# Delta rule and MoE in one kernel: three copies instead of four for a chunk's answers, halved last outputs, and a new order of issue

## The chip, the cores and the metric

The kernel runs on one core of a Trainium2 chip. The metric is the device time of one execution in microseconds (us); lower is better. Kernels are compared by medians over executions on the same chip. One execution was also recorded by the hardware profiler; it has a time of its own, and a span from its first to its last instruction.

## What is computed

The reference is a linear attention layer with the delta rule, followed by a two-layer MoE expert whose inputs are the attention's outputs:

```python
def _attn_ref(q, k, v, beta):                 # 4 batches, 8 heads, 768 tokens, 48 channels
    k_n = k / (np.linalg.norm(k, axis=-1, keepdims=True) + 1e-06)
    for t in range(S):
        y[:, :, t] = np.einsum('bhd,bhde->bhe', q[:, :, t], state)
        v_old = np.einsum('bhde,bhd->bhe', state, kt)
        state = state + bt[:, :, :, None] * np.einsum('bhd,bhe->bhde', kt, vt - v_old)
...
def _moe_ref(x, w_in, w_out):                 # 3072 tokens, 384 -> 2048 -> 384
    h = x @ w_in
    g = h - np.tanh(h)
    return (g @ w_out).astype(np.float32)
```

## The kernel before

**Tiling.** The 768 tokens of a sequence are cut into 24 chunks `s` of 32; the 4 batches lie in the four quadrants of 32 partitions. Four chunks make a group `g` for the triangular solve and also a window `w` of 512 tokens for the MoE, so there are six of each.

**The recurrent part.** For the first four chunks `head` (L469) forms products of keys on TensorE straight from an early load `kf`; for later chunks `score` (L500) forms them, with the queries' products beside them, from tiles `kc` or `kd`. `solve(g)` inverts the triangular system of a group on VectorE: a transpose (L538), a row of small operations, thirty pairs of multiply and add (L594, L596), a scaling (L599) and a transpose (L604) that gives `tt`. VectorE also scales the values of the first four chunks (`prep`, L621, `wv<-v`). `chain` then goes from chunk to chunk: keys against the state (L642), the solution applied (L663), its copy `u_sb` (L671), the state's update (L679, L706), the answers (L692). `output` brings a chunk's answers from two PSUM banks to `y_sb` in four copies of 32 partitions on ScalarE (L719), because the answer of quadrant `b` lies in quadrant `b^1` of bank `b%2`; TensorE transposes them (L729) into `psa`, and two reads of it (L733 on ScalarE, L735 on VectorE) leave the high and low parts in `xt`.

**The MoE.** A unit of `hidden` is nine matmuls (L838), one of `out_units` nine more (L888); between them `gate` runs two operations on ScalarE and two on VectorE. A unit covers 512 tokens, except that the first `F0` feature blocks of the first window are done in two halves of 256 tokens, so that they can begin when two chunks are there. The weights come as 16 pieces: loaded as `raw` and decoded by ScalarE and VectorE (L750, L773, L786, L789). For the first ten pieces TensorE forms the low part, in two halves per piece of a matmul on `c` (L795) and one on `w` (L796), which ScalarE copies out (L799).

**The order.** Python simulates the engines while it emits code. `Plan.run` picks the next operation by earliest start and due time, from tables of costs and the numbers at the file's end (`QUIRK`, `OPEN` and so on). Each engine then runs its instructions in the order they were emitted. Where the plan sees TensorE idle, `warm` emits a matmul on a tile of zeros (L356, `po<-wz`); it computes nothing. `burn` does the same at the very start with `BURN` small matmuls (L333). The plan also counts TensorE's instructions in blocks of 256 (`fetched`, `fetch`), starting from the number `taken`. Loads are issued by SyncE in the order of `FIRST`, the later weights by ScalarE's queue.

**The end.** `finish` copies the three banks of a window (ScalarE, VectorE, ScalarE; L907) into a tile `o` that has two buffers, and stores each with one DMA (L910).

Of the kernel before, what the change touches and what calls it, by code (L numbers as in the profile page):

```python
# [8 lines left out]
F32 = mybir.dt.float32  # L9
F32R = mybir.dt.float32r  # L10
# [20 lines left out]
KR = 112  # L31
SPLIT = ((0, 0), (0, 1), (1, 0))
HALF = (slice(0, 48), slice(64, 112))


class Null:
# [208 lines left out]


def act(n, psum=False):
    return (0.17 if psum else 0.19) + 0.82e-3 * n


# [9 lines left out]
def kernel(ctx: ExitStack, tc: tile.TileContext, kf, kq, vk, beta, w_in, w_out, const, out):  # L260
# [118 lines left out]
    def load_values(s):  # L379
        both = ld.tile([128, 2, H, D], F32, name="v", bufs=VS)  # L380
        nc.sync.dma_start(both, vk[s])
        v_of[s] = (both, transfer(plan.free["SP"], 384), rv.take())

    beta_of = {}
    rbt = Ring(2)
# [243 lines left out]
    def chain():  # L629
        for s in range(NS):  # L630
# [2 lines left out]
            g, r = divmod(s, 4)  # L633
            solution = lambda: made[s].t if s in made else None
            if s > 0:
                (_, t) = yield Op("PE", 0.68, (known(kd_of, s, 1), get(s, "v", 2), state[s - 1], rk), by - 8.0, "small", 128)
# [73 lines left out]
    def output(s, py, pyr, e):  # L710
# [2 lines left out]
        y_sb = at.tile([128, DM], F32, tag="uy", name="y_sb", bufs=UYS)  # L713
        yr = ruy.take()
        yv = y_sb.rearrange("p (h e) -> p h e", h=H)
        for b in range(4):
            if b:
                (_, t) = yield Op("ACT", act(DM, True), (e,), need(s) - 3.0)
            nc.scalar.copy(yv[quad[b]], py[quad[b ^ 1], b % 2])  # L719
# [8 lines left out]
        for ct in range(NC):  # L728
            nc.tensor.transpose(px[:, ct, :], y_sb[:, 128 * ct:128 * ct + 128], ident)  # L729
# [142 lines left out]
    def out_units(units):  # L872
        for w, f, part, z in units:
# [9 lines left out]
            count = NF + F0 if w == 0 else NF  # L883
            po = pos[w][0]
            gh, gr = gh_of.pop((w, f, z))
            for c in range(NC):
                for i, (a, b) in enumerate(SPLIT):
                    nc.tensor.matmul(po[c][:, part], wo[f][:, a, 128 * c:128 * c + 128], gh[:, b, :n],  # L888
                                     start=(f == 0 and i == 0 and z < 1), stop=(ended.get(w, 0) == count - 1 and i == 2),
                                     skip_group_check=True)  # L890
            gr.t = t
            ended[w] = ended.get(w, 0) + 1
            if ended[w] == count:
# [2 lines left out]
    ended = {}  # L896
    ros = Ring(2)

    def finish(w, e):
        po, por = pos[w]  # L900
        t = 0.0
        for c in range(NC):
            eng = ("ACT", "DVE", "ACT")[c]
            (_, t1) = yield Op(eng, act(T, True) if eng == "ACT" else dve(T), (e, ros, closed), start(w + 1) - 4.0)
            o = post[0].tile([128, T], F32, name="o", bufs=2)
            orr = ros.take()
            (nc.scalar.copy if eng == "ACT" else nc.vector.tensor_copy)(o, po[c])  # L907
            t = max(t, t1)
            (_, t2) = yield Op("SP", ISSUE, (Event(t1),), start(w + 1) - 4.0)
            nc.sync.dma_start(out[w, c], o)  # L910
            orr.t = transfer(t2, 256).t
        por.t = t
# [46 lines left out]
    return plan  # L959


QUIRK = {'piece13': 15, 'prep0': 3, 'output0': -1, 'out_units0.0.1': 73, 'decode9': -28, 'hidden0.-1.2': 35, 'vsub0': -27, 'piece15': 75, 'solve0': 8, 'solve1': 5, 'piece4': -8, 'score1': -14, 'hidden0.1.3': -45, 'gate0.1.3': 17, 'vsub1': 13, 'out_units0.-1.3': 40, 'piece6': -10, 'out_units0.-1.1': -5, 'score2': -8, 'mask2': 40, 'score4': -20, 'piece11': 32, 'hidden0.0.3': 17, 'piece9': -5, 'decode5': 62, 'gate0.1.0': -7, 'chain5': -24, 'vsub4': 5, 'out_units0.1.1': -13, 'piece14': 54, 'join5': 13, 'decode12': -37, 'hidden0.0.2': 12, 'mask4': -15, 'add3': -18, 'piece10': -5, 'join4': 35, 'prep2': -28, 'output1': -30, 'mask5': -28, 'score0': 7, 'gate0.-1.0': -35, 'piece5': -22, 'answer2': 4, 'decode3': -15, 'chain3': -25, 'output5': -8, 'decode14': -15, 'add6': -35, 'piece12': -38, 'piece8': -17, 'answer3': 68, 'score3': 0, 'chain6': -10, 'answer5': 45, 'join0': -5, 'mask1': 15, 'add5': 22, 'out_units0.0.0': -30, 'out_units0.1.3': 14, 'output6': 24, 'prep1': 8, 'add1': -28, 'gate0.1.1': -7, 'decode1': -20, 'decode10': 8, 'decode0': -5, 'answer1': -3, 'mask3': 0, 'piece7': -15, 'mask0': -5, 'add4': -15, 'answer0': 17, 'hidden0.-1.0': 0, 'answer7': 22, 'add2': 5, 'add0': -5, 'decode2': -10, 'output2': -10, 'decode11': -18, 'out_units0.1.2': 0, 'vsub7': -12, 'output3': -4, 'hidden0.0.0': -7, 'solve2': 2, 'hidden0.-1.1': 10, 'hidden0.1.2': 22, 'chain1': -27, 'join7': -2, 'prep5': -15, 'vsub2': -5, 'gate0.-1.2': 10, 'output4': 2, 'vsub3': -2, 'chain4': 20, 'decode15': -5, 'chain7': -5, 'decode4': -20, 'join3': 5, 'mask6': -8, 'out_units0.1.0': 20, 'hidden0.1.1': -5, 'score7': 7, 'gate0.0.0': -10, 'decode8': -2, 'triangle1': 20, 'join6': 10, 'hidden0.0.1': -10, 'score6': 2, 'output7': -2, 'vsub5': -18, 'prep4': 10, 'decode13': 20, 'gate0.0.1': -10, 'chain0': -5, 'join1': 20, 'gate0.0.2': -2}
# [3 lines left out]
OPEN, SECOND, EARLY, PITCH, SPREAD, URGENCY, FETCH, QUEUED, FILL, LEAD, STICK = 87.5, 184.8, 44.6, 80.0, 13.6, 0.012, 3.8, 3.0, 150.0, 18.4, 0.0  # L966
WARM, HOLD, GUARD, F0 = 90.0, 120.0, 0.28, 4
FIRST = ['f0', 'f1', 'f2', 'f3', 'b0', 'w0', 'w4', 'k2', 'k1', 'v2', 'k3', 'v3', 'k0', 'w3', 'b1', 'k4', 'k6', 'w1', 'w2', 'v0', 'k7', 'v1', 'k5']
WHIM, SEED = 0.0, 199030
FIRST_NEED, NEXT_NEED, EAGER, JOIN = 42.9, -27.4, -269.8, -52.4  # L970
LOW, SPARE, MARGIN = True, 10, 15.2
# [60 lines left out]
```

## Time and profile before

| what | value |
|---|---|
| median of 3 runs | 610.96 us (610.93 to 611.75) |
| the profiled execution's own time | 610.21 us |
| its span, first to last instruction | 608.5 us |
| TensorE matmul busy | 97% of the span |
| VectorE, ScalarE, GpSimd busy | 64%, 42%, 10% |
| granted TensorE clock, mean | 0.995 |

A row of the timeline has its start and duration in us, the engine and line, the operation, the tiles written and read, a count where instructions were merged, and in brackets the idle time before it with what ended it. TensorE's high busy share has two readings: some of it is the matmuls on zeros that the plan put where it expected to wait.

### The profile page before, as it was taken

To read this page: it belongs to the slowest core of one execution; us is meant where nothing else is said; L and a number is where in the kernel's file an instruction comes from. 1 tells how busy PE (TensorE), PEld (TensorE's weight loads), DVE (VectorE), ACT (ScalarE), POOL (GpSimd) and SP (SyncE) were. 2 spreads that over 40 slices of the span, in tenths; PEclk is the share of its full clock that TensorE was granted. 3 is DMA by queue.
4 is the path that set the end of the run, shared out by engine and by line. 5 is a ranking of instruction groups with operands and counts; after the bars stand their busy time and mean duration, and the time that the engine had idled before them with its cause. 6 is when DMAs were issued, how large, how long until landed. Compare 5 with 4: busy or idle time off the path is not lost.

```text
span 608.5 us, 21905 instructions
## 1 busy us (share of the span) xinstructions
PE 588.2 (97%) x9984; PEld 459.7 (76%) x9984; DVE 390.5 (64%) x826; ACT 257.9 (42%) x472; POOL 58.6 (10%) x60
## 2 busy tenths in 40 slices
PE   4799999999999999999999999999999999999996
PEld 3355677978788878778878778877788877788885
DVE  2988768898478986789334789732779733243323
ACT  2243877656354244353243433334444235432223
POOL 0111010001021031010011200000200000000000
PEclk9899999999999999999999999999999999999999
DMA  8842466533222133232032231021121000010001
GB/s 282 342 161 95 141 206 197 165 106 124 85 79 77 71 110 122 65 96 75 14 97 70 92 98 52 1 90 37 53 74 52 3 2 3 3 52 1 0 1 52
DMA packets 19436, 52.44 MB, mean 86 GB/s; under 512 B 2576, under 2 KB 2704, under 8 KB 19344
## 3 DMA queue, kind: packets, MB, share of 16 engines
q1 hardware_dynamic: 15840, 43.10, 20.9%
q10 hardware_dynamic: 3504, 7.95, 4.1%
q8 instruction: 78, 1.28, 0.8%
q14 instruction: 14, 0.11, 0.1%
HBM read 46.32 MB, written 4.72 MB: 84 GB/s over the span
## 4 chain that ended last, share of the span: by engine, by line
PE 89%; DVE 4%; ACT 3%; DMA 2%; issue 2%; ACTq 0%
PE ph L838 32%; PE po L888 31%; PE po L356 4%; PE psk L642 4%; PE psa L500 4%; PE psa L663 3%; PE psk L692 3%; PE psa L679 2%; PE ph L795 2%; PE psa L729 1%; DMA raw<-in_w_in 1%; ACT y_sb L719 1%; PE ph L679 1%; DMA kc<-in_kq 1%; DVE c L786 1%
## 5 line engine op out<-in xcount | busy, mean ns | idle before, releaser
L888 PE MATMUL po<-gh,w 128*128 128x512 f32 (+1 forms) x900 | 213.7, 387 | 0.3 <-DVE gh L865 0.3
L838 PE MATMUL ph<-xt,w 128*128 128x512 f32 (+1 forms) x900 | 213.2, 387 | 0.2 <-DVE tmp L594 0.2
L888 PEld LDWEIGHTS po<-gh,w 128*128 128x128 f32 x900 | 161.7, 188 | 34.3 <-DVE gh L865 0.6
L838 PEld LDWEIGHTS ph<-xt,w 128*128 128x128 f32 x900 | 161.4, 188 | 34.1 <-DVE tmp L594 0.7
L855 ACT ACTIVATE t<-ph 128x512 f32<-128x512 f32 (+1 forms) x100 | 58.1, 581 | 149.1 <-PE ph L838 138.3
L857 DVE TENSOR_TENSOR t<-ph,t 128x512 f32<-128x512 f32 (+1 forms) x100 | 66.8, 668 | 82.1 <-ACT t L855 81.8
L865 DVE TENSOR_TENSOR gh<-t,gh 128x512 fp32r<-128x512 f32 (+1 forms) x100 | 69.2, 692 | 42.4 <-ACT gh L863 41.2
L863 ACT CAST gh<-t 128x512 fp32r<-128x512 f32 (+1 forms) x100 | 60.4, 604 | 75.0 <-DVE t L857 37.0
L596 DVE TENSOR_TENSOR a<-a,tmp 128x30 f32<-128x30 f32 (+9 forms) x180 | 62.5, 347 | 5.1
L594 DVE TENSOR_TENSOR tmp<-a 128x30 f32<-128x30 f32 (+9 forms) x180 | 62.3, 346 | 4.7
L719 ACT COPY y_sb<-psk 32x384 f32<-32x384 f32 x96 | 45.2, 471 | 37.0 <-PE psk L692 36.0
L621 POOL TENSOR_TENSOR wv<-v,nt 128x768 f32<-128x768 f32 x20 | 30.8, 1543 | 213.7 <-PE psa L663 169.3
L356 PE MATMUL po<-wz 128*128 128x512 bf16 x148 | 38.0, 393 | 0.0
L517 POOL TENSOR_TENSOR pq<-pq,cs 128x256 f32<-128x256 f32 x24 | 19.3, 802 | 160.6 <-ACT pq L511 160.6
L735 DVE TENSOR_TENSOR xt<-psa,xt 128x384 fp32r<-128x384 f32 x24 | 13.3, 555 | 27.7 <-ACT xt L733 27.7
L642 PEld LDWEIGHTS psk<-st,kd 48*64 48x64 f32 x1472 | 23.6, 134 | 5.2 <-issue 4.2
L642 PE MATMUL psk<-st,kd 48*64 48x48 f32 x1472 | 26.4, 220 | 0.0
L356 PEld LDWEIGHTS <-wz 128*128 128x128 bf16 x148 | 13.3, 99 | 16.6 <-issue 3.7
L651 DVE TENSOR_TENSOR wv<-wv,psk 128x768 f32<-128x768 f32 x23 | 21.9, 951 | 5.2 <-PE psk L642 4.4
L663 PEld LDWEIGHTS psa<-wv,tt 32*32 32x32 f32 x1536 | 17.9, 105 | 8.6 <-issue 5.8
L679 PEld LDWEIGHTS psa<-u_sb,v 32*48 32x48 f32 x736 | 18.3, 119 | 7.9 <-issue 6.5
L500 PEld LDWEIGHTS psa<-kc 48*32 48x32 f32 x1344 | 19.4, 107 | 5.7 <-issue 3.9
(70 smaller groups left out, 454.6 us busy)
## 6 DMA issues: line engine op xcount, KB each, us to landing
kd<-in_kq SPq DMA_DIRECT2D x23, 512.0 KB, 3.5
kc<-in_kq SPq DMA_DIRECT2D x21, 512.0 KB, 4.0
v<-in_vk SPq DMA_DIRECT2D x24, 384.0 KB, 3.7
out<-o SPq DMA_DIRECT2D x18, 256.0 KB, 2.0
raw<-in_w_in ACTq DMA_DIRECT2D x5, 768.0 KB, 6.0
raw<-in_w_out ACTq DMA_DIRECT2D x5, 768.0 KB, 4.6
raw<-in_w_in SPq DMA_DIRECT2D x3, 768.0 KB, 9.3
raw<-in_w_out SPq DMA_DIRECT2D x3, 768.0 KB, 10.2
```

The costliest lines, as they stand in the source:

```text
L356: nc.tensor.matmul((ps if own else pos[w][0][0]).rearrange("p (a b) -> p a b", a=4), wz, wide, start=own, stop=own, skip_group_check=not own)
L500: nc.tensor.matmul(ps[quad[b], h, :], k[:, z], k[:, 1 - z] if g == 0 else k[:, ::-1] if z else k, start=True, stop=True)
L594: nc.vector.tensor_tensor(tv, a[:, j + 1:, j:j + 1].broadcast_to(shape), a[:, j:j + 1, :j].broadcast_to(shape), ALU.mult)
L596: nc.vector.tensor_tensor(a[:, j + 1:, :j], a[:, j + 1:, :j], tv, ALU.add)
L642: nc.tensor.matmul(pk[64 * pr:64 * pr + 64, z, h, :], kd[HALF[z], 2 * h + pr].rearrange("p a c -> p (a c)"), st[HALF[z], pr, h, :], start= ...
L719: nc.scalar.copy(yv[quad[b]], py[quad[b ^ 1], b % 2])
L838: nc.tensor.matmul(p, wi[f][:, a, ct, :], xt[:, b, ct, part], start=(ct == 0 and i == 0), stop=(ct == NC - 1 and i == 2))
L855: nc.scalar.activation(t_, p, AF.Tanh)
L857: nc.vector.tensor_tensor(t_, p, t_, ALU.subtract)
L863: nc.scalar.copy(gh[:, 0, :n], t_)
L865: nc.vector.tensor_tensor(gh[:, 1, :n], t_, gh[:, 0, :n].bitcast(F32), ALU.subtract)
L888: nc.tensor.matmul(po[c][:, part], wo[f][:, a, 128 * c:128 * c + 128], gh[:, b, :n], start=(f == 0 and i == 0 and z < 1), stop=(ended.get( ...
```

## The change

A chunk's answers leave their banks in three copies: one of all 128 partitions from bank 1, which is right for two quadrants, then two of 32 partitions from bank 0 for the other two. Chunk 0 keeps four copies. The quadrants stay where the banks have them (`b^1`), and the two reads behind the transposes put them in order with a reversed access pattern. In the last window the third bank's final three matmuls are done in two halves of 256 tokens, and `last` copies four parts (two of 512, two of 256) into a tile that has no second user and stores each by itself. `BURN` goes from 48 to 44, one group of four small matmuls fewer; `F0` from 4 to 6; `taken`, slacks, due times, the order of loads and `QUIRK` change as well, which makes the plan emit another order.

```diff
-    SLACK = {"PE": 0.112, "DVE": 2.784, "ACT": 0.062, "POOL": 0.2, "SP": 0.0}
+    SLACK = {"PE": 0.115, "DVE": 1.502, "ACT": 0.05, "POOL": 0.2, "SP": 0.0}
...
-        self.taken, self.loaded, self.coming, self.arrived, self.crossed = 62, 512, None, 0.0, 0.0
+        self.taken, self.loaded, self.coming, self.arrived, self.crossed = 70, 512, None, 0.0, 0.0
...
-        for b in range(4):
-            if b:
+        moves = [(slice(0, 128), 1), (quad[1], 0), (quad[3], 0)] if s else [(quad[b], 1 - b % 2) for b in range(4)]
+        for k, (rows, x) in enumerate(moves):
+            if k:
                 (_, t) = yield Op("ACT", act(DM, True), (e,), need(s) - 3.0)
-            nc.scalar.copy(yv[quad[b]], py[quad[b ^ 1], b % 2])
+            nc.scalar.copy(yv[rows], py[rows, x])
...
-        xh = xt[:, 0, :, 128 * z:128 * z + 128]
+        px = px.rearrange("p c (g x i) -> p c g x i", x=2, i=C)[:, :, :, ::-1]
+        side = lambda x: xt[:, x, :, 128 * z:128 * z + 128].rearrange("p c (g x i) -> p c g x i", x=2, i=C)
+        xh = side(0)
...
-        nc.vector.tensor_tensor(xt[:, 1, :, 128 * z:128 * z + 128], px, xh.bitcast(F32), ALU.subtract)
+        nc.vector.tensor_tensor(side(1), px, xh.bitcast(F32), ALU.subtract)
...
+                pieces = ENDS if final and w == NW - 1 and c == NC - 1 else (slice(0, n),)
...
+    def last(po, e):
+        o = mo.tile([128, 2, NC, T], F32R, tag="xt0", name="ends", bufs=1).bitcast(F32)[:, 0]
+        parts = [(c, slice(0, T)) for c in range(NC - 1)] + [(NC - 1, x) for x in ENDS]
+        for k, (c, x) in enumerate(parts):
+            eng = ("ACT", "DVE")[k % 2]
...
+            (nc.scalar.copy if eng == "ACT" else nc.vector.tensor_copy)(o[:, c, x], po[c][:, x])
+            (_, t) = yield Op("SP", ISSUE, (Event(t),), 0.0)
+            nc.sync.dma_start(out[NW - 1, c][:, x], o[:, c, x])
...
-BURN, LATCH = 48, ((8, 1), (8, 2))
+BURN, LATCH = 44, ((8, 2),)
...
-WARM, HOLD, GUARD, F0 = 90.0, 120.0, 0.28, 4
-FIRST = ['f0', 'f1', 'f2', 'f3', 'b0', 'w0', 'w4', 'k2', 'k1', 'v2', 'k3', 'v3', 'k0', 'w3', 'b1', 'k4', 'k6', 'w1', 'w2', 'v0', 'k7', 'v1', 'k5']
+WARM, HOLD, GUARD, F0 = 90.0, 150.0, 0.22, 6
+FIRST = ['f0', 'f1', 'f2', 'f3', 'b0', 'w4', 'k3', 'v2', 'k0', 'k2', 'w0', 'k1', 'v3', 'k7', 'k6', 'b1', 'w3', 'k4', 'w1', 'w2', 'v0', 'v1', 'k5']
...
-AHEAD, BEHIND = 6, 1
+AHEAD, BEHIND = 5, 1
```

Three places show how the order moves. First, TensorE's queue at the program's start, as it was (L333 is `burn`, L469 the four `head` groups, L356 a matmul on zeros with its weight load, L500 a `score`):

```order
L333 MATMUL psa_87<-wz_84 32x16 x48
L469 MATMUL psa_87<-kf0_97 32x32 x32
L469 MATMUL ph0_89<-kf1_115 32x32 x32
L469 MATMUL ph1_90<-kf2_133 32x32 x32
L469 MATMUL psa_87<-kf3_147 32x32 x32
L356 LDWEIGHTS wz_84
L356 MATMUL po0_92<-wz_84 128x512
L500 MATMUL psa_87<-kd2_230 32x32 x32
```

And as it is now (the lines are numbered by the changed file; L336 is `burn`, L473 `head`, L359 a matmul on zeros):

```order
L336 MATMUL psa_87<-wz_84 32x16 x44
L473 MATMUL psa_87<-kf0_97 32x32 x32
L473 MATMUL ph0_89<-kf1_115 32x32 x32
L473 MATMUL ph1_90<-kf2_133 32x32 x32
L473 MATMUL psa_87<-kf3_147 32x32 x32
L359 LDWEIGHTS wz_84
L359 MATMUL po0_92<-wz_84 128x512
```

Four small matmuls are gone ahead of the heads, and five matmuls on zeros (the first is shown) stand ahead of the first score instead of one.

Second, VectorE in the first solve, behind the scaling of `a` that precedes the thirty pairs. Before, the first weight piece (`c`, `lo`, L786) came straight behind it:

```order
L583 SCALAR_TENSOR_TENSOR a_323<-a_323,gm 128x1024
L786 SCALAR_TENSOR_TENSOR c_331<-c_331,lo_333 128x768
L594 TENSOR_TENSOR tmp<-a_323 128x30
L596 TENSOR_TENSOR a_323<-a_323,tmp 128x30
L594 TENSOR_TENSOR tmp<-a_323 128x58
```

Now it comes two pairs later (L587 is the scaling, L598 and L600 the pairs, L793 the weight piece):

```order
L587 SCALAR_TENSOR_TENSOR a_314<-a_314,gm 128x1024
L598 TENSOR_TENSOR tmp<-a_314 128x30
L600 TENSOR_TENSOR a_314<-a_314,tmp 128x30
L598 TENSOR_TENSOR tmp<-a_314 128x58
L600 TENSOR_TENSOR a_314<-a_314,tmp 128x29x2
L793 SCALAR_TENSOR_TENSOR c_382<-c_382,lo_388 128x768
```

Later in the same solve the two scalings of values and two more weight pieces stand close together (L625 is `prep`):

```order
L598 TENSOR_TENSOR tmp_675<-a0_314 128x220
L793 SCALAR_TENSOR_TENSOR c1_658<-c1_658,lo1_665 128x768
L600 TENSOR_TENSOR a0_314<-a0_314,tmp_675 128x11x20
L625 TENSOR_TENSOR wv_690<-v_569,nt_321 128x768
L625 TENSOR_TENSOR wv_725<-v_575,nt_321 128x768
L598 TENSOR_TENSOR tmp_735<-a0_314 128x210
L600 TENSOR_TENSOR a0_314<-a0_314,tmp_735 128x10x21
L793 SCALAR_TENSOR_TENSOR c2_678<-c2_678,lo2_727 128x768
```

Before, that solve held two weight pieces and two scalings of values, 12 rows apart; the third piece followed behind its last transpose.

Third, SyncE's loads behind the four early key loads, as they were (`raw0` is the first weight piece):

```order
L389 DMA bt_157<-in_beta 128x32
L404 DMA raw0_224<-in_w_in 128x3x512
L404 DMA raw4_226<-in_w_in 128x3x512
L364 DMA kd2_230<-in_kq 128x1024
L364 DMA kd1_232<-in_kq 128x1024
L381 DMA v_234<-in_vk 128x768
L364 DMA kd3_236<-in_kq 128x1024
```

And as they are now:

```order
L393 DMA bt_153<-in_beta 128x32
L408 DMA raw4_220<-in_w_in 128x3x512
L367 DMA kd3_222<-in_kq 128x1024
L384 DMA v_226<-in_vk 128x768
L367 DMA kc0_228<-in_kq 128x1024
L367 DMA kd2_230<-in_kq 128x1024
L408 DMA raw0_232<-in_w_in 128x3x512
```

The first weight piece has moved behind `raw4` and four tiles of keys and values.

More of the change, by code (lines that the diff above doesn't have):

```diff
@@ L33 @@
 HALF = (slice(0, 48), slice(64, 112))
+ENDS = (slice(0, T // 2), slice(T // 2, T))
 class Null:
@@ L381, in load_values @@
         nc.sync.dma_start(both, vk[s])
-        v_of[s] = (both, transfer(plan.free["SP"], 384), rv.take())
+        e = transfer(plan.free["SP"], 384)
+        v_of[s] = (both, Event(e.t + SLOW * (e.t < 60.0)), rv.take())
     beta_of = {}
@@ L885, in out_units @@
             gh, gr = gh_of.pop((w, f, z))
+            final = ended.get(w, 0) == count - 1
             for c in range(NC):
[L887 to L890, printed above, removed]
+                pieces = ENDS if final and w == NW - 1 and c == NC - 1 else (slice(0, n),)
+                for x in pieces:
+                    for i, (a, b) in enumerate(SPLIT):
+                        nc.tensor.matmul(po[c][:, part][:, x], wo[f][:, a, 128 * c:128 * c + 128], gh[:, b, x],
+                                         start=(f == 0 and i == 0 and z < 1), stop=(final and i == 2),
+                                         skip_group_check=True)
             gr.t = t
@@ L897 @@
     ros = Ring(2)
+    def last(po, e):
[3 more added lines that the diff above has]
+            eng = ("ACT", "DVE")[k % 2]
+            n = x.stop - x.start
+            (_, t) = yield Op(eng, act(n, True) if eng == "ACT" else dve(n), (Event(e.t - (1.4, 0.7, 0.35, 0.0)[k]), closed), 0.0)
+            (nc.scalar.copy if eng == "ACT" else nc.vector.tensor_copy)(o[:, c, x], po[c][:, x])
+            (_, t) = yield Op("SP", ISSUE, (Event(t),), 0.0)
+            nc.sync.dma_start(out[NW - 1, c][:, x], o[:, c, x])
     def finish(w, e):
         po, por = pos[w]
+        if w == NW - 1:
+            yield from last(po, e)
+            return
         t = 0.0
```

14 lines of the change are left out of this document (8 added, 6 removed).

## Prediction

> **What bounds the kernel now.** I read the page's busy line first, then TensorE's windows, then the chain at the start and at the end. A row of the windows gives the stretch, its length, and the busy time of PE, PEld, DVE, ACT and POOL.
>
> ```profile
> PE 588.2 (97%) x9984; PEld 459.7 (76%) x9984; DVE 390.5 (64%) x826; ACT 257.9 (42%) x472; POOL 58.6 (10%) x60
> 58.00:130.00 72.00, 70.36 (x1439) 54.54 (x1438) 55.32 (x129) 49.57 (x93) 6.09 (x6) 1.00 0.53 167
> 130.00:540.00 410.00, 409.80 (x7282) 327.80 (x7281) 271.13 (x568) 170.37 (x316) 44.79 (x40) 1.00 0.19 62
> ```
>
> From 130 to 540 us TensorE is busy 409.80 of 410 us; between 58 and 130 it misses 1.64 us. So the end is set by when the steady work can begin, by how much TensorE is given behind that point, and by what follows its last matmul. I take the three apart. The mark between the first two is the first use of a solution (L663), which needs the whole first solve:
>
> ```profile
> 14.44 0.31 PE L469 MATMUL psa<-kf 48*32 48x32 f32 x2 [4.39 <-issue]
> 14.78 0.60 DVE L474 COPY gs<-psa 128x256 f32<-128x256 f32 x1 [4.92 <-PE psa L469]
> 54.71 1.95 DVE L604 STREAM_TRANSPOSE tt<-a 128x1024 f32<-128x1024 f32 x1
> 57.90 0.88 PE L663 MATMUL psa<-wv,tt 32*32 32x48 f32 x64
> ```
>
> Two of the last head's matmuls wait 4.39 us for "issue" and only then can VectorE begin the solve. It has `tt` at 56.66, and TensorE, still on its matmuls on zeros, uses it at 57.90.
>
> **The headline edit.** A copy of 32 partitions costs what one of 128 does:
>
> ```profile
> L719 ACT COPY y_sb<-psk 32x384 f32<-32x384 f32 x96 | 45.2, 471 | 37.0 <-PE psk L692 36.0
> L671 ACT COPY u_sb<-psa 128x384 f32<-128x384 f32 x24 | 11.5, 481 | 10.1 <-PE psa L663 10.0
> 65.50 0.55 PE L729 MATMUL psa<-cs,y_sb 128*128 128x128 f32 x3 [1.08 <-ACT y_sb L719]
> ```
>
> So 23 chunks save one copy of 0.47 us each, 10.8 us of ScalarE. On the path it is worth **nothing**: the one wait of TensorE for `y_sb` is that of chunk 0, which keeps its four copies, and everywhere else the full TensorE covers it. Were the cover gone, a chunk would gain 0.47 us. The permuted reads of `psa` have no row of their own; the nearest pair is a copy of 256 elements in a reordered and in a plain form:
>
> ```profile
> L507 ACT COPY gs<-psa 128x256 f32<-128x256 f32 x20 | 12.6, 632 | 18.5 <-PE psa L500 18.4
> L511 ACT COPY pq<-psa 128x256 f32<-128x256 f32 x24 | 9.9, 412 | 4.1 <-PE psa L500 4.1
> ```
>
> The 0.22 us between them, for 384 elements 0.33 us, is the upper bound; nothing is the lower, because the innermost run stays 32 elements. On 24 chunks and two engines that is 0 to 8 us each, beside the same TensorE: nothing. I take 0.
>
> **The start.** The chain's beginning counts instructions (start, us, line, number; the first row is a group's, the last the queue's):
>
> ```profile
> L333 PE MATMUL psa<-wz 32*32 32x16 f32 x96 | 1.7, 211 | 2.0 <-DVE idle L317 1.1 <-DVE psa L325 1.0
> 3.69 1.02 PE psa L469 x64
> 4.71 0.96 PE ph L469 x63
> 5.67 2.33 issue
> 8.00 1.20 PE ph L469 x65
> 9.20 0.85 PE psa L469 x62
> q8 instruction: 78, 1.28, 0.8%
> ```
>
> The instruction queue moved 78 packets, and 9984 matmuls with 9984 weight loads are 19968 instructions: 256 to a packet. Between the two stalls stand 65 + 62 = 127 pairs, 254 instructions. The second stall is thus a block's end, falling four instructions before the heads are done. Each of the four small matmuls that `burn` loses is two pairs (its 48 show as 96), so 16 instructions go, the heads end 12 before the block's end, and the five matmuls on zeros fill those. **The stall then falls on the first score, not on the solve**: the heads end near 10.0, VectorE starts the solve 4.7 us earlier.
>
> The Trainium skill's "Runtime: NRT & Kernel Launch", section "Instruction fetch mechanics", has blocks of 256 instructions too, but says that crossing a boundary costs one tail-bump of a DMA and is mostly hidden. Here 4.39 us are not hidden; by that sentence the idle time would be something else and need not move (the first rival).
>
> What is late next:
>
> ```profile
> 12.56 0.89 ACT L750 ACTIVATE c<-raw 128x768 f32<-128x768 f32 x1 [8.44 <-DMA kd<-in_kq]
> 10.00:15.00 5.00, 0.61 (x6) 0.28 (x3) 0.22 (x1) 1.11 (x2) 0.00 (x0) 1.00 1.04 399
> 14.78 0.90 ACT L773 ACTIVATE lo<-raw 128x768 int32<-128x768 uint8 x1 [1.33 <-PE psa L469]
> 22.17 1.23 DVE L583 SCALAR_TENSOR_TENSOR a<-a,gm 128x1024 f32<-128x1024 f32 x1
> 40.75 0.96 DVE L621 TENSOR_TENSOR wv<-v,nt 128x768 f32<-128x768 f32 x1 [2.22 <-DMA v<-in_vk]
> ```
>
> The first weight piece was there at 12.5. Now 768 + 512 + 384 + 512 + 512 KB, 2.75 MB, go ahead of it; at 399 GB/s (the last column of the window) that is 6.9 us, so it lands at 19.4, its two ScalarE steps take 0.9 us each, and VectorE can take it at 21.2. VectorE comes there, behind the scaling (22.17 + 1.23 - 4.7 = 18.7) and two pairs of some 0.9 us, at 19.7: it waits 1.5 us. TensorE's matmul on that piece can start near 22.1. The third weight piece inside the solve adds 0.9 us; the wait of 2.22 us for values goes if they land by 38.5, though their loads are now queued on SyncE behind a key load that needs a buffer from a score. VectorE alone would have `tt` at 56.66 - 4.7 + 1.5 + 0.9 - 2.2 = 52.2.
>
> But TensorE comes later than that, as it does before:
>
> ```profile
> 25.00:30.00 5.00, 5.00 (x137) 2.77 (x137) 4.48 (x14) 1.46 (x4) 0.85 (x1) 0.66 0.68 255
> 24.31 0.91 PE L795 MATMUL ph<-c,cs 128*128 128x384 f32 x2 [3.91 <-DVE c L786]
> 50.09 7.88 PE po L356 x36
> 62.28 0.91 PE L795 MATMUL ph<-c,cs 128*128 128x384 f32 x2
> 64.03 0.39 PE L356 MATMUL po<-wz 128*128 128x512 bf16 x1
> ```
>
> A matmul on zeros takes 7.88 / 36 = 0.22 us, and a piece's low part 64.03 - 62.28 = 1.75 us. That piece started at 24.31. From it to the first use of the solution the order has 98 of the former before and 89 now, one piece more, and the same seven scores: 57.90 - 24.31 - 1.97 + 1.75 = 33.4 us, less some 1.2 us because the clock, granted 0.66 from 25 to 30 behind the wait of 3.91 us (1.7 of 5 us), should fall less behind a shorter one. 22.1 + 32.2 = 54.3. The term is **-3.6 us**; its bounds are 52.2 (VectorE alone, -5.7) and 57.5 (no gain from the stall, -0.4).
>
> **Behind the first use.** TensorE's sum by the order's counts:
>
> ```profile
> L356 PE MATMUL po<-wz 128*128 128x512 bf16 x39 | 11.0, 383 | 0.0
> 521.27 2.27 PE ph L838 x9
> 536.20 2.04 PE ph L838 x9
> 79.06 1.26 PE ph L838 x9
> 86.99 1.07 PE po L888 x9
> ```
>
> Zeros: 38 before in the order (39 in the row, whose window cuts one), 30 now: 8 x 0.22 = -1.75 us. One weight piece less, since it now lies ahead of that step: -1.75. A unit between wide units is 2.04 us of the chain, one behind narrow work (here L642) 2.27. The runs of wide work behind narrow work fall from 93 to 88: 5 x 0.23 = -1.15. With `F0` = 6, eight half units of 1.07 to 1.26 us stand for four whole ones of 2.04 to 2.27: +0.9 with the split at the end, between +0.2 and +1.2. Sum **-3.7 us**. Waits that the plan doesn't see were 1.64 + 0.20 us before and are taken as the same; nothing shows them for the new order, and they may be 0 or several us.
>
> **The end.**
>
> ```profile
> 597.39 4.77 PE po L888 x21
> 602.87 0.69 DVE L907 COPY o<-po 128x512 f32<-128x512 f32 x1 [2.05 <-PE po L888]
> 602.81 3.07 SPq L910 DMA_DIRECT2D out<-o  x3
> 604.93 0.59 ACT L907 COPY o<-po 128x512 f32<-128x512 f32 x1 [2.15 <-DMA out<-o]
> ```
>
> The last matmul ends E = 603.5 (the second copy starts three matmuls, 0.68 us, before it). The third copy waits for the first store to free its buffer, and its own store is issued at 605.52, E + 2.0; the three issues end at 605.88, so one takes 0.36. Now no buffer is shared; a copy of 256 ends near E + 0.45, but SyncE issues the last three stores one behind another at 0.36 us each from E + 0.05: the last at E + 0.77. The term is **-1.25 us** (-0.9 to -1.6).
>
> **Sum.** -3.6 - 3.7 - 1.25 = -8.55 us. The profiled execution would take 610.21 - 8.55 = 601.66; its median lies 0.75 us above it, so 610.96 - 8.55 = 602.4.
>
> **The rivals.**
>
> *The stall does not move* (chance 0.13). For: what ends it is not named, only "issue". Against: the 254 instructions. VectorE then starts as before and reaches the weight piece two pairs later, at 24.3, without a wait; TensorE's part begins at 25.3, and 25.3 + 32.2 = 57.5, so the start is worth 0.4: 610.96 - 0.4 - 3.7 - 1.25 = 605.6. If it is hidden, as the skill's sentence has it, and the idle time is another's, this is the outcome.
>
> *New waits eat the gain* (0.07). The start is earlier, but weights and values are not:
>
> ```profile
> raw<-in_w_in ACTq DMA_DIRECT2D x5, 768.0 KB, 6.0
> 112.73 6.00 DMA raw<-in_w_in
> ```
>
> A weight load is on the chain of before at 112.73, with 6.00 us. If the units ahead of it are done 7.3 us earlier and it is not, TensorE waits up to 7.3 us there: 602.4 + 7.3 = 609.7, within 0.2% of before.
>
> *Slower* (0.09). The same place, one step worse: one weight fewer is loaded ahead (`AHEAD` 5), so the late pieces come one load of 6.00 us later as well, 602.4 + 7.3 + 6.0 = 615.7 if all shows, and 612.5 if about half is covered by units of other pieces. It decides from 9.8 us of new waits on (0.2% past the median). Against: half units from six blocks instead of four need fewer pieces early.
>
> **How the numbers follow.** The forecast has 0.71, with 599.5 to 605 as its own range: the start's -5.7 would give 600.3, the other terms' spreads are some 1 us, new waits up to 2.5 us. A measurement can tell about 0.2%, 1.2 us, from no change. Faster 0.71 + 0.13 and a hundredth of the second rival's: 0.85; same 0.06; slower 0.09. The range goes to 607 to take in the first rival and leaves out the last two.
>
> **What would show it.** The idle time "issue" of 4.39 us at L469 gone and one like it at the first score; the transpose that begins the solve near 10.7 instead of 15.42; the first use of a solution near 54.3; 30 matmuls on zeros behind it; three stores close together at the end. TensorE's idle time between 55 and 130 above 4 us, on weights or values, would make the forecast wrong; so would a first use of a solution after 56.

## The result, and the profile after

| | before | after |
|---|---|---|
| median (lowest to highest), six runs each | 611.36 us (610.59 to 613.46) | 608.57 us (607.29 to 610.32) |
| the profiled execution's own time | 610.21 us | 607.97 us |
| its span | 608.5 us | 606.3 us |

The ratio is 0.9949, with a 95% interval of 0.9925 to 0.9973: faster by 0.5%, or 2.8 us, where 8.6 were forecast. The range ended at 607 us; 608.57 lies above it.

The span splits at the two marks of the prediction, the first use of a solution and the last matmul's start. The middle comes from the windows of each kernel between its own marks, the last from the page's span.

| stretch | before | after | change | predicted |
|---|---|---|---|---|
| span's start to first use of a solution | 57.90 | 58.03 | +0.13 | -3.6 |
| first use to the last matmul's start | 545.23 | 544.17 | -1.06 | -3.7 |
| last matmul's start to the span's end | 5.37 | 4.06 | -1.31 | -1.25 |

The timeline of TensorE and VectorE in the changed kernel, from the heads to the first use (L473 is `head`, L542 and L608 the solve's first and last transpose, L504 `score`, L625 the scaling of values, L802 a weight piece's low part, L667 the first use):

```profile
7.83 1.01 PE L473 MATMUL ph<-kf 48*32 48x32 f32 x58 [1.64 <-issue]
8.60 1.09 PE L473 MATMUL psa<-kf 48*32 48x32 f32 x64
10.35 1.25 DVE L542 STREAM_TRANSPOSE a<-gs 128x1024 f32<-128x1024 f32 x1
14.10 0.75 PE L504 MATMUL psa<-kd 48*32 48x32 f32 x64 [2.16 <-DVE z L568]
19.79 0.96 DVE L793 SCALAR_TENSOR_TENSOR c<-c,lo 128x768 int32<-128x768 int32 x1 [0.52 <-ACT lo L780]
20.80 0.91 PE L802 MATMUL ph<-c,cs 128*128 128x384 f32 x2 [0.71 <-DVE c L793]
42.02 1.10 PE L504 MATMUL psa<-kc 48*32 48x64 f32 x64 [3.83 <-DMA kc<-in_kq]
43.05 0.61 PE L359 MATMUL po<-wz 128*128 128x512 bf16 x1
46.88 1.10 PE L504 MATMUL psa<-kc 48*32 48x64 f32 x64
39.66 1.93 DVE L625 TENSOR_TENSOR wv<-v,nt 128x768 f32<-128x768 f32 x2 [2.12 <-DMA v<-in_vk]
50.54 1.97 DVE L608 STREAM_TRANSPOSE tt<-a 128x1024 f32<-128x1024 f32 x1
58.03 0.66 PE L667 MATMUL psa<-wv,tt 32*32 32x48 f32 x43
```

The heads run without the 4.39 us, VectorE begins the solve at 10.35 and has `tt` at 50.54 + 1.97 = 52.51, 4.2 us earlier than before. TensorE uses it 5.5 us later. The first score, at 14.10, waits 2.16 us. The row names VectorE's `z`; the same wait is put down to `nm` of L576 in the run with room for keys below, so the name is not to be relied on. The score starts behind 349 matmuls, where the prediction's count puts the end of a block. One row stands out: the score at 42.02, which waits 3.83 us for its keys. The chain that ended last goes through that load:

```profile
30.79 1.07 PE psa L504 x64
31.88 10.00 DMA kc<-in_kq
```

The load was issued at 31.88, right behind the score before it, whose buffer it takes, and took 10.00 us. SyncE's issues say why so long:

```profile
27.05 0.33 SPq L367 DMA_DIRECT2D kc<-in_kq  x1
27.43 1.17 SPq L405 DMA_DIRECT2D raw<-in_w_out  x1
28.64 0.47 SPq L408 DMA_DIRECT2D raw<-in_w_in  x1
29.16 0.97 SPq L384 DMA_DIRECT2D v<-in_vk  x2
31.88 0.33 SPq L367 DMA_DIRECT2D kc<-in_kq  x1
```

Until 27.05 the queue stood still behind a key load that needed the buffer of an earlier score. Then 512 + 768 + 768 + 2 x 384 KB went out, and the keys of that score, those of chunk 5, behind them. Matmuls at 43 to 46 are slow besides; the window of that stretch (its length, busy times of PE, PEld, DVE, ACT and POOL, the granted clock, DMA share, GB/s) shows the clock at one half:

```profile
43.00:46.00 3.00, 3.00 (x15) 1.69 (x7) 2.76 (x9) 1.31 (x4) 0.00 (x0) 0.50 0.49 158
```

In the middle, the windows of after, and below them the sum of the matching windows of before, between its own marks:

```profile
58.03:130.00 71.97, 70.97 (x1475) 57.52 (x1475) 58.18 (x135) 47.05 (x91) 5.93 (x6) 1.00 0.49 162
130.00:540.00 410.00, 407.68 (x7277) 328.42 (x7276) 277.57 (x568) 160.38 (x296) 44.74 (x40) 1.00 0.19 62
...
sum 544.17, PE 540.54 PEld 436.68 DVE 356.41 ACT 226.19 POOL 50.67; mean PE 180.18 PEld 145.56 DVE 118.80 ACT 75.40 POOL 16.89
```

```profile
sum 545.23, PE 543.39 PEld 434.69 DVE 348.55 ACT 240.13 POOL 50.88; mean PE 181.13 PEld 144.90 DVE 116.18 ACT 80.04 POOL 16.96
```

TensorE's work fell by 2.85 us, but its idle time rose from 1.84 to 3.63. From 130 to 540, where 0.20 us were idle before, it is now 2.32, and two scores hold nearly all of that:

```profile
301.09 0.88 PE L696 MATMUL psk<-u_sb,pq 32*32 32x48 f32 x64
301.90 1.02 PE L504 MATMUL psa<-kc 48*32 48x64 f32 x57
304.28 0.31 PE L504 MATMUL psa<-kc 48*32 48x64 f32 x7 [1.36 <-issue]
...
326.19 0.30 PE L504 MATMUL psa<-kc 48*32 48x64 f32 x4 [0.84 <-issue]
```

Each stops inside a group of 64 matmuls that belong together, for "issue", as the head did before.

### The profile page after: what moved, and what is told of

It reads as the page before. It is cut to its first block, busy times and chain, and to the rows that moved or that the text cites. A ratio compares the mean times of both kernels' runs of the same rounds, so it can differ in the third digit from the quotient of the medians.

```text
span 606.3 us, 21901 instructions
## 1 busy us (share of the span) xinstructions
PE 588.3 (97%) x10007; PEld 462.9 (76%) x10007; DVE 399.2 (66%) x831; ACT 247.3 (41%) x453; POOL 58.4 (10%) x60
## 4 chain that ended last, share of the span: by engine, by line
PE 92%; DMA 3%; DVE 2%; ACT 1%; issue 1%; SPq 1%; ACTq 0%
PE ph L845 34%; PE po L898 33%; PE psk L646 4%; PE psa L504 4%; PE po L359 3%; PE psk L696 3%; PE psa L667 3%; PE ph L802 3%; PE psa L683 2%; DMA kc<-in_kq 2%; DMA raw<-in_w_in 2%; PE psa L734 1%; PE ph L683 1%; PE ph L803 1%; DVE a L600 0%
## 5 line engine op out<-in xcount | busy, mean ns | idle before, releaser
L598 DVE TENSOR_TENSOR tmp<-a 128x30 f32<-128x30 f32 (+9 forms) x180 | 64.9, 361 | 4.8
L600 DVE TENSOR_TENSOR a<-a,tmp 128x30 f32<-128x30 f32 (+9 forms) x180 | 63.4, 352 | 5.2
L625 POOL TENSOR_TENSOR wv<-v,nt 128x768 f32<-128x768 f32 x20 | 31.0, 1552 | 185.7 <-PE psa L667 185.7
L724 ACT COPY y_sb<-psk 32x384 f32<-32x384 f32 (+1 forms) x73 | 34.5, 473 | 32.5 <-PE psk L696 31.5
L359 PE MATMUL po<-wz 128*128 128x512 bf16 x140 | 37.4, 407 | 0.0
L504 PE MATMUL psa<-kc 48*32 48x64 f32 (+1 forms) x1344 | 23.2, 216 | 6.1 <-DMA kc<-in_kq 3.8
L504 PEld LDWEIGHTS psa<-kc 48*32 48x32 f32 x1344 | 19.7, 107 | 10.5 <-issue 8.7
L359 PEld LDWEIGHTS <-wz 128*128 128x128 bf16 x140 | 13.2, 102 | 17.3 <-issue 5.5
L667 PEld LDWEIGHTS psa<-wv,tt 32*32 32x32 f32 x1536 | 17.9, 105 | 8.4 <-issue 5.1
```

The source lines that it names most:

```text
L359: nc.tensor.matmul((ps if own else pos[w][0][0]).rearrange("p (a b) -> p a b", a=4), wz, wide, start=own, stop=own, skip_group_check=not own)
L504: nc.tensor.matmul(ps[quad[b], h, :], k[:, z], k[:, 1 - z] if g == 0 else k[:, ::-1] if z else k, start=True, stop=True)
L598: nc.vector.tensor_tensor(tv, a[:, j + 1:, j:j + 1].broadcast_to(shape), a[:, j:j + 1, :j].broadcast_to(shape), ALU.mult)
L600: nc.vector.tensor_tensor(a[:, j + 1:, :j], a[:, j + 1:, :j], tv, ALU.add)
```

## The experiments

Two theories of the start stood at the outset. In one the stall's move was worth what was forecast, and the wait for keys, with the clock behind it, took it back. In the other the first use is held by something else, so that neither stall nor keys decide. For the middle, the theory was that idle time put down to "issue" comes where narrow groups in a row use up 256 instructions faster than the next ones arrive. All ratios are to the kernel before, on the same chip. Line numbers shift by a few with each edit.

### Room for two more key tiles

The keys of chunks 4 and 5 go into a tile that nobody uses yet, so that neither they nor the loads right behind them wait for a score's buffer. In the changed kernel:

```diff
+        if tag == "kc" and s in (4, 5):
+            if not spare:
+                spare.append(mo.tile([128, 2, NC, T], F32R, tag="xt0", name="spare", bufs=1).bitcast(F32).rearrange("p a c t -> p (a c t)"))
+            k = (4, 5).index(s)
+            kc = spare[0][:, 1024 * k:1024 * k + 1024].rearrange("p (u a c) -> p u a c", u=16, a=2)
+        else:
+            kc = ld.tile(...)
```

> The changed kernel, same order on every engine, but the keys of chunks 4 and 5 are loaded into memory that the first window's activations use only later, so SyncE need not wait for a score before it issues them and the loads behind them. Theory A (the gain of the start was lost to the late keys of chunk 5: TensorE waited 3.8 us for them at 42.0 and ran 3.4 us at half clock behind that): the wait goes, the first use of the solution comes at 53.3 to 55 instead of 58.1, the time falls by 3.5 to 5 us against the changed kernel, to about 0.987 of before. Theory B (the start is bound elsewhere, by values or weights, and the keys only show it): the first use moves by less than 1 us and the time by less than 1 us.

And in the kernel before, with the same edit for chunks 7 and 5:

> The kernel before with the same room for two key tiles (chunks 7 and 5, those that waited there), same order. Theory A: VectorE's wait of 2.2 us for values goes, but TensorE is bound by its own matmuls up to the first use of the solution (57.9), so the time changes by less than 0.8 us. Theory B (the start is bound by loads before as well): 2 us faster or more.

The changed kernel ran in 605.01 us, ratio 0.9885 (0.9866 to 0.9904). TensorE's timeline, where `spare` is the new tile:

```profile
40.21 1.10 PE L510 MATMUL psa<-spare 48*32 48x64 f32 x64
41.24 0.39 PE L359 MATMUL po<-wz 128*128 128x512 bf16 x1
43.44 1.10 PE L510 MATMUL psa<-kc 48*32 48x64 f32 x64
54.59 0.88 PE L673 MATMUL psa<-wv,tt 32*32 32x48 f32 x64
```

The score that waited until 42.02 comes at 40.21 without a wait. From the matmul on zeros behind it to the next score it takes 43.44 - 41.24 = 2.20 us, against 46.88 - 43.05 = 3.83 at half clock: 1.63 us. **The first use comes at 54.59**, 3.44 us earlier than in the changed kernel and 0.3 from the predicted 54.3. The score's earlier start (1.81 us) and the whole clock behind it (1.63) make up that difference. The second theory of the start falls.

The kernel before ran in 609.96 us, 0.9972 (0.9957 to 0.9987). Its own score waited 0.26 us for such keys, and its first use, at 58.24, comes no earlier. The time fell by 0.3%, about 1.7 us, all the same, where less than 0.8 was expected; the profiled execution, at 610.55 among the slower of its eight, does not show where, and that stays open. For the first use the old order of loads did not need the room; the new one does.

### The stall put back

The four small matmuls return, so that the block's end falls on the heads again. The rest of the change stays, without and with the room for keys:

```diff
-            for rows in quad:
+            for rows in quad + quad if i == 1 else quad:
```

> The changed kernel with the four small matmuls put back at the start, everything else in the same order, so that the end of the instruction block falls on the last head again. Theory A: the solve begins at about 14.8 to 15.4 again instead of 10.35, and the time changes by less than 1 us, since TensorE waits for the keys of chunk 5 anyhow. Theory C (the stall's move did bring its 4.4 us and something else lost it again): 3.5 to 4.5 us slower than the changed kernel.

> Both: room for the two key tiles and the four small matmuls put back. Theory A: with the keys there in time the block's end on the last head costs 3 to 4.5 us, so this is that much slower than with room for keys alone, and about as fast as the changed kernel. Theory B and C: the four small matmuls cost less than 1 us here or the same as without the room.

Without the room: 616.91 us, 1.008 (1.0057 to 1.0102). With it: 611.59 us, 0.9997 (0.9979 to 1.0015). The timeline of the first:

```profile
15.14 0.31 PE L473 MATMUL psa<-kf 48*32 48x32 f32 x2 [5.22 <-issue]
47.36 1.93 PE L504 MATMUL psa<-kc 48*32 48x64 f32 x64 [2.66 <-ACT lo L780]
63.32 0.88 PE L667 MATMUL psa<-wv,tt 32*32 32x48 f32 x63
```

The stall is where it was, as two of the heads' matmuls show, and costs more than either theory had expected: 8.3 us against the changed kernel, and with the room for keys 6.6 us. In the profiled execution without the room 5.3 us of that lie ahead of the first use and 2.9 in the middle (547.10 us against 544.17). A late transfer does not swallow it, because the loads themselves wait for scores, and the scores come behind the stall: the late score moves from 42.02 to 47.36. What ended its wait here is ScalarE's work on a weight piece; that piece's load was issued at 35.06, behind the same held key load that went out at 27.05 in the changed kernel and at 33.57 now. The first use of a solution, in the six profiled executions:

| order of issue | stall at the heads | stall moved off |
|---|---|---|
| before | 57.90 | 54.37 |
| changed | 63.32 | 58.03 |
| changed, room for keys | 58.63 | 54.59 |

(54.37 is the next run's.) In each row the stall is worth 3.5 to 5.3 us. From the first row to the second, **the new order of issue costs 3.7 to 5.4 us**; the room gives 3.4 to 4.7 of it back, so that most of this cost lies in the loads. The two effects cancel in these executions of the change.

Each value is one execution's, and they scatter. The runs with four copies and with the old end, further down, have the changed kernel's instructions up to the first use, and there it came at 57.22 and 55.83. The score on chunk 5's keys waited 2.41 and 2.24 us instead of 3.83; in the second no half clock followed. Against the one execution with room, at 54.59, the late keys with the clock behind them thus cost 1.2 to 3.4 us. In all, the room is worth 3.6 us by the medians.

### The old order without the stall

The kernel before, with four small matmuls fewer and nothing else:

```diff
-            for rows in quad:
+            for rows in quad if i < 11 else ():
```

> The kernel before with nothing changed but the number of small matmuls that are emitted at the start, 44 instead of 48. Theory A: the heads end near 10.0, the solve begins near 10.5 instead of 15.4 and the first use of the solution comes at 53 to 55 instead of 57.9; the time falls by 3 to 4.5 us, if later blocks of instructions bring no new waits. Rival: another load or weight is late in turn and the first use moves by less than 1 us, as it did in the change.

605.64 us, 0.9907 (0.9879 to 0.9935).

```profile
8.49 1.09 PE L469 MATMUL psa<-kf 48*32 48x32 f32 x64
54.37 0.88 PE L663 MATMUL psa<-wv,tt 32*32 32x48 f32 x64
```

The last head is one group of 64, unbroken, and the first use comes 3.53 us earlier, although the first score now waits 5.64 us for its keys. Sixteen instructions less are worth 0.93%, or 5.7 us, where 3 to 4.5 were expected; in the profiled execution the middle, too, is 1.0 us shorter (544.20 us). The whole change, which holds them, is worth 0.51%. The intervals of the two overlap a little, so that this shows only that the rest of the change adds nothing to it that can be measured.

### Another four small matmuls fewer

For the middle: the changed kernel with room for keys and 40 small matmuls at the start instead of 44. Every block's end behind them moves by 16 instructions.

```diff
-            for rows in quad:
+            for rows in quad if i < 10 else ():
```

> The changed kernel with room for the two key tiles and 40 instead of 44 small matmuls at the start, order otherwise the same: 16 instructions fewer ahead of everything, so that every later block of 256 ends 16 instructions further on in the work. Theory D (the two scores near 302 and 324 us that took 1.6 and 1.1 us too long wait for the next block of instructions, because three narrow groups in a row use up a block faster than one arrives): both waits go and no new one over 1 us comes, 2 to 2.7 us faster than with the room alone. Theory E (those waits have another cause, a semaphore or the keys): the same within 0.5 us.

603.28 us, 0.9866 (0.9843 to 0.9889). The score that stopped near 300 us in the run with 44:

```profile
298.14 0.88 PE L702 MATMUL psk<-u_sb,pq 32*32 32x48 f32 x64
298.95 1.10 PE L510 MATMUL psa<-kc 48*32 48x64 f32 x64
```

It runs through. The middle takes 542.30 us instead of 543.39 with the same room and 44 small matmuls. The medians differ by 1.7 us where 2 to 2.7 were expected, and the two intervals overlap. All four profiled executions with 44 and the new order of issue (two more follow) show both broken scores, the first with 1.0 to 1.4 us of idle time; none of the five with 40 does. But the first of the two waits has not gone; it has moved into the `out` unit behind the score and grown shorter:

```profile
301.33 2.00 PE L904 MATMUL po<-gh,w 128*128 128x512 f32 x8 [0.85 <-issue]
```

Counted through the traces, it stands behind the same number of TensorE's matmuls as before, 5832, whatever the group there: the score's last 15 matmuls with 48 small ones at the start (both runs with the stall put back), its last 7 with 44, eight of the unit's nine with 40 (three of five, 0.58 to 0.85 us). The second stands behind 6342 in all six runs of the new order with 48 or 44. The waits near the start stand behind 222 or 223 matmuls (in the heads, in every run), 349 or 350 and 604. From one of these five places to the next are multiples of 127 to 127.5 matmuls, each with its weight load: blocks of 256 instructions, but for one or two. The block theory holds for these waits, and a shift by 16 instructions changes which group a block's end hits, not whether there is one.

### Four copies again, and the old end

In `output` of the changed kernel, the copy of 128 partitions is done as two of 32:

```diff
-            nc.scalar.copy(yv[rows], py[rows, x])
+            for r in (quad[0], quad[2]) if s and not k else (rows,):
+                nc.scalar.copy(yv[r], py[r, x])
```

> The changed kernel with four copies per chunk again, in the same places of ScalarE's order (the first copy split into its two quadrants). Theory A (the headline edit is hidden behind TensorE): ScalarE busier by 23 x 0.47 = 10.8 us, the time within 0.5 us of the changed kernel. Rival: the third copy's absence shortens the path to the transposes, 1 us or more slower here.

608.95 us, 0.9961 (0.9935 to 0.9986), against 0.9949 (0.9925 to 0.9973) with three: not to be told apart. TensorE's waits (line, what it waited for, us in total, times, longest):

```profile
PE psa L735 <- ACT y_sb L725: 1.1, 2, 0.7
```

The changed kernel has no such wait. That is the most the headline edit can be shown to give: **1.1 us of 610** in this order. The permuted reads of `psa`, for which up to 0.33 us each was allowed, cost nothing: 479 ns on ScalarE and 554 on VectorE (means), against 480 and 555 before.

For the end, the changed kernel with whole matmuls and without `last`:

```diff
-                pieces = ENDS if final and w == NW - 1 and c == NC - 1 else (slice(0, n),)
+                pieces = (slice(0, n),)
...
-        if w == NW - 1:
-            yield from last(po, e)
-            return
```

> The changed kernel with the old end: no halved matmuls, three whole copies into the tile of two buffers. Theory A: the third copy waits for a store again, 1.0 to 1.4 us slower than the changed kernel. Rival (the halves cost what the shared buffer cost): no difference.

607.23 us, 0.9933 (0.9909 to 0.9958): 1.3 us below the changed kernel by the medians, where 1.0 to 1.4 more were expected. The intervals overlap, and the time does not show the edit beside the spread of the rest; in its profiled execution the first use came at 55.83 instead of 58.03. But the stretch behind the last matmul's start does: 5.34 us, as before (5.37), against 4.06. Its third copy waits for a store again, 2.14 us.

### The third bank in one piece

The run with 40 small matmuls, with a tile of its own for the last outputs but no halves:

```diff
-        parts = [(c, slice(0, T)) for c in range(NC - 1)] + [(NC - 1, x) for x in ENDS]
+        parts = [(c, slice(0, T)) for c in range(NC)]
```

> The changed kernel with room for two key tiles and 40 small matmuls at the start, with the last window's third bank in one piece: no halved matmuls, three copies and three stores, still into a tile of its own. If the tile of its own is what shortened the end and the halves' copies wait for one another, the time from the last matmul's start to the end of the span stays at 4.06 us or falls by up to 0.4, and three short matmuls fewer stand ahead of it: in all 0 to 0.6 us faster than the run before (603.28). If halving is what shortened it, that stretch grows by 0.2 to 0.5 us.

602.65 us, 0.986 (0.9838 to 0.9881), where that run has 0.9866 (0.9843 to 0.9889). The end of the changed kernel, and then of this one:

```profile
601.74 2.11 SPq L918 DMA_DIRECT2D out<-ends  x4
...
602.52 0.37 ACT L916 COPY ends<-po 128x256 f32<-128x256 f32 x1 [0.80 <-PE po L898]
602.92 0.42 DVE L916 COPY ends<-po 128x256 f32<-128x256 f32 x1 [0.42 <-ACT ends L916]
```

```profile
596.41 1.69 SPq L924 DMA_DIRECT2D out<-ends  x3
...
597.16 0.58 ACT L922 COPY ends<-po 128x512 f32<-128x512 f32 x1 [0.77 <-PE po L904]
```

The two half copies run one behind the other, 602.52 to 603.34, and need a fourth store. From the last matmul's start to the span's end the whole bank takes 4.12 us and the halves 4.06. The gain at the end is the tile of its own; the halves give nothing.

### Fewer matmuls on zeros

With the room for keys and 40 small matmuls, `tt` is there at 51.35 and used at 55.30: TensorE is on matmuls on zeros. In that run, 14 of the 22 in a row were replaced by 7 tiny ones, and in a second kernel by nothing:

```diff
+            zeros.append(0)
+            if 92 < len(zeros) <= 106:
+                if len(zeros) % 2:
+                    nc.tensor.matmul(ps[:32, :16], wz.bitcast(F32)[:32, :32], wz.bitcast(F32)[:32, :16], start=True, stop=True)
+                continue
```

> The changed kernel with room for two key tiles and 40 small matmuls at the start (the run before it: 603.28 us, first use of a solution at 55.30 us while the solution was ready at 51.35), and 14 of the 22 matmuls on zeros ahead of that first use replaced by 7 tiny matmuls, so that the count of instructions behind them stays. Zeros that the plan put there for a later solution hold the first use: it comes 14 x 0.22 - 7 x 0.05 = 2.7 us earlier, near 52.5, and the time is near 600.5 us, 0.982 of the kernel before. Rival: the zeros only fill a wait for weights, values or keys, which then shows as idle time; the first use moves by less than 0.5 us and the time stays at 603.

> As the run with fewer matmuls on zeros, but with nothing in their place: 28 instructions fewer ahead of everything behind the first use, 14 fewer than with the tiny matmuls in place. If waits for blocks of 256 instructions hang on where the blocks' ends fall, the first use comes as early as there (or 0.3 us earlier), but the stretch from it to the last matmul is 2 to 4 us longer, with idle time put down to issue at two or more narrow groups. Rival: what counts there is only the number of matmuls; the stretch is the same within 0.5 us.

With the tiny ones: 601.09 us, 0.9827 (0.9807 to 0.9847). TensorE's timeline of the run with 22 zeros, and then of this one, with the window of its slow stretch:

```profile
29.77 3.84 PE L359 MATMUL po<-wz 128*128 128x512 bf16 x17
33.54 1.10 PE L510 MATMUL psa<-spare 48*32 48x64 f32 x64
55.30 0.88 PE L673 MATMUL psa<-wv,tt 32*32 32x48 f32 x64
```

```profile
29.43 0.39 PE L516 MATMUL psa<-kc 48*32 48x32 f32 x23 [2.02 <-issue]
29.75 5.53 PE L365 MATMUL po<-wz 128*128 128x512 bf16 x17
35.21 1.10 PE L516 MATMUL psa<-spare 48*32 48x64 f32 x64
54.60 0.88 PE L679 MATMUL psa<-wv,tt 32*32 32x48 f32 x64
```

```profile
29.80:33.20 3.40, 3.40 (x12) 1.20 (x10) 3.16 (x8) 0.37 (x1) 0.72 (x1) 0.50 0.97 368
```

From the first score on `spare` to the first use the stretch shrank from 21.76 to 19.39 us, 2.37 of the 2.7 expected. But the same 17 zeros ahead of that score took 5.53 instead of 3.84 us, at half clock, so that in the profiled execution only 0.7 us of it arrive. The zeros did hold the first use.

With nothing in their place: 599.13 us, 0.9805 (0.9775 to 0.9835). Here the theory of the blocks expected 2 to 4 us more in the middle, and **that failed**. Its profiled execution, the slowest of its four, shows one new wait in the middle, in a group of a chunk's answers,

```profile
99.99 0.28 PE L708 MATMUL psk<-u_sb,pq 32*32 32x48 f32 x4 [1.07 <-issue]
```

and a middle of 542.58 against 542.01, 0.6 us more. The wait stands behind 2133 matmuls, again at a block's end by the count above; what failed is the number and the size of such waits. Ahead of the first use this execution waited 2.98 us inside its first score, which the one with tiny matmuls did not.

### All of it together

Room for keys, 40 small matmuls, 14 zeros left out, the third bank whole:

> The run with 14 zeros left out and the run with the third bank in one piece put together: room for two key tiles, 40 small matmuls at the start, 14 matmuls on zeros fewer ahead of the first use, three whole copies at the end. If the parts add, the ratio to the kernel before is 0.980 or less (0.9805 of the one, and nothing to 0.4 us of the other), near 599 us, with a first use of a solution near 53 where TensorE's clock stays whole behind the block's end at the score of the fifth chunk (54.2 with the clock halved there). Rival: the earlier run's median of 599.1 us was four lucky executions, and this one lies with the tiny matmuls' run, at 601.

**599.3 us, 0.9809 (0.9795 to 0.9823)**: faster than both kernels, and the earlier median was no luck. 0.980 or less was expected if the parts add, which the interval allows; the first use came at 54.23, as expected for a clock halved at the score near 30 us, and it was. Its middle, from the windows:

```profile
sum 540.42, PE 539.72 PEld 436.31 DVE 356.76 ACT 227.68 POOL 51.15; mean PE 179.91 PEld 145.44 DVE 118.92 ACT 75.89 POOL 17.05
```

Behind the first use its instructions are those of the run before but for the end, and the wait of 1.07 us is not there: some of these waits come and go between executions.

## Why the prediction was wrong

**The start: half right, and the failed step is here.** That the stall ends a block, that sixteen instructions less carry it off the heads and onto the first score were right: the solve begins at 10.35 (10.7 predicted), the weight piece is waited for 0.52 us (1.5), TensorE's part starts at 20.80 (22.1). That `tt` comes at 52.51 (52.2) is in part luck: the wait of 2.2 us for values was taken as gone if they land by 38.5, but VectorE was there at 37.54 and waited 2.12 us, until 39.66; the rest of its row was 1.8 us shorter than summed. That did not decide, as `tt` was still there first. The failed step is the sum from there to the first use, 32.2 us: it counted TensorE's matmuls and took the transfers between them as they were. It came to 58.03 - 20.80 = 37.23. The wait for chunk 5's keys, a term put at nothing, is 3.83 us of that and the half clock behind it 1.63, together 5.46 against 5.03 too many. With room for those keys the first use came at 54.59. How much the step cost varies: in the two other executions of these instructions the wait was 2.41 and 2.24 us and the first use at 57.22 and 55.83. The prediction had seen that the values stand behind a key load that waits for a score, but not that the next keys stand behind the values and two weight pieces. Its clock term, a gain of 1.2 us from a shorter wait, missed that a new wait brings its own.

**Behind the first use: work right to 0.9 us, waits wrong.** TensorE's work fell by 2.85 us where 3.7 were summed, and the waits, taken as the same, grew by 1.79. Two broken scores account for 2.20 us of idle time. They were in reach: the start's stall had shown that a block's end stops a narrow group, and the new order was there to count. With four small matmuls fewer again one is gone and the other shorter, and in the last run the middle is 540.42, 4.8 us below before.

**The end: right.** -1.31 against -1.25, and the old end brings 5.34 back. The cause was the shared buffer, as said. The halves were worth nothing: the sum had taken their two copies as done side by side, and they ran one behind the other.

**The headline edit: right within what can be measured.** Nothing was forecast; at most 1.1 us shows.

**The rivals.** The measured 608.57 lies by the second rival's 609.7, whose mechanism is the right kind and the wrong place: not a weight load near 112 us, as TensorE is idle for 1.00 us between 58.03 and 130, but keys at 42 and blocks at 302 and 324. A first use after 56, which the prediction named as a sign of being wrong, came in this execution at 58.03.

## What to carry to other kernels

When work moves earlier, write down for each load ahead of it when its buffer comes free and how many bytes stand before it in its queue: a sum of one engine's work is only a lower bound. Count instructions to the block's end before and after an edit at the front, since a few more or less move every later end into another group. And look at matmuls that compute nothing: once their reason has moved, they hold what they were to bridge.

## What was not expected of the hardware

**Waits for a block of instructions.** The ends of blocks of 256 instructions on TensorE's queue cost 4.1 to 5.2 us where they fell on the last head, 0.5 to 3.0 inside the first score, 1.6 to 2.0 at a score near 29 us, 0.5 to 1.6 at scores in the middle, and once 2.67 in a unit of 256-token matmuls (at 82.97, the stall put back, with room for keys). The Trainium skill's "Runtime: NRT & Kernel Launch", section "Instruction fetch mechanics", calls the crossing mostly hidden; in these kernels that holds for most of the 78 blocks; where it does not, groups of short matmuls mostly follow one another. Why the same order waits in one execution and not in the next stays open.

**The clock.** The idle time of 2.02 us at the score of 29.43 was followed by 3.4 us at half clock, and so were 2.00 and 2.03 us there in the next two runs with fewer zeros; 1.56 to 1.75 us at the same score in three other runs were not, yet 1.55 us ahead of 310.10 in the run with the stall put back was. The Trainium skill's "TensorE: Matmul & The Clock Gate", in "Part 1: The HAM clock gate", puts the halving behind an idle window of about 3.4 us; the traces show it behind less. In the run with fewer zeros that cost 5.53 - 3.84 = 1.7 us beyond the wait's own length. The column of the granted clock does not show all of it. In the run with 44 small matmuls and room for keys, behind its wait of 2.62 us at the first score, the timeline and a window:

```profile
15.50 6.13 PE L359 MATMUL po<-wz 128*128 128x512 bf16 x16
```

```profile
16.00:18.00 2.00, 2.00 (x6) 0.66 (x5) 1.97 (x4) 0.00 (x0) 0.72 (x1) 1.00 1.05 409
```

The column has 1.00, but a matmul on zeros takes 6.13 / 16 = 0.38 us there instead of 0.22, some 2.6 us on the 16.
